# Eight deep visits: VectorE's order around the second layer's first four sums

## The chip, the cores and the metric

The kernel runs on one core of one Trainium2 chip. The metric is the device time of one execution in microseconds (us), lower is better. Three executions of the kernel before took 889.67, 889.99 and 894.23 us, median 889.99.

## The reference

Linear attention by random features, followed by a mixture of four two-layer experts in which every expert sees every token.

```python
# attention, per batch b and head h (4 x 8, 576 tokens, head size 64, 128 features)
phi(x) = exp(h - max(h)) / sqrt(m),   h = x @ omega.T - sum(x * x) / 2
kv = einsum('bhsm,bhsd->bhmd', phi(k), v);  z = sum(phi(k), axis=2)
out = (phi(q) @ kv) / (phi(q) @ z + 1e-6)

# experts: x is the attention output, 2304 tokens x 512; E = 4, F = 1024
p = probs / (probs.sum(-1) + 1e-9)
for e in range(E):
    out += p[:, e] * (relu(x @ w1[e]) @ w2[e])
```

## The kernel before, in words

Every float32 operand of a matmul is split into a high and a low part, and each product is three matmuls (high x high, high x low, low x high), which add up in PSUM. The work on the experts goes in *visits*: one visit takes one half of one expert's hidden units (eight halves in all) for one block of tokens. The last eight visits take the last block, 1024 tokens; the code calls them DEEP, and in them both layers are computed with seven block products in place of eight (a Strassen-like scheme). The function `fast(v)` writes a visit. The attention of later batches lies beside the earlier visits and is over by then.

The order on each engine is the order in which the code writes the instructions; no scheduler changes it, and waits are semaphores that follow from the tiles read and written. Two instructions on one PSUM bank by TensorE and VectorE are put in order too, even if they touch different halves of it.

A deep visit has two parts.

The first layer is 14 products (`p1` to `p7` for two groups g) of six matmuls, 128x512 each. `p4(1)`, the last one, ends with a ReLU whose high part ScalarE writes (L922) and whose low part VectorE writes (L925, `hl`). `both` adds a product to an earlier sum (L879) and writes low parts (L892).

The second layer, in `sevens()`, is seven groups of 24 matmuls, 128x256 each, six for each of four token tiles q. Four PSUM banks `X[q]` have a left half L and a right half R; two more banks hold `zs`. In TensorE's order the groups are:

- G1: L of X, from `hs[:2]` (laid between p7, p3 and p4 of the first layer)
- G2: R of X, from `T1`, added to what L's bank already holds
- G3: `zs`, from `hs[2:]`; its sixth matmul is the first that needs the low half `hl` of p4
- G4: R of X, from `A22`
- G5: L of X, from `hs[:2]`, written anew by ScalarE and GpSimd from `t2`
- G6: L of X, from `hs[2:]`, written anew from `r11`
- G7: L of X, from `T1`, written anew from `t1`

Because each group adds to what the bank holds, VectorE must have read a half of X[q] before the next group on this bank may write there: `gather` (L714 or L718) multiplies the half by the token's probability and adds it to an accumulator. `second(q)` is a gather of `zs`, `third(q)` one of R after G4.

Between them stand the differences that make the next operands, written by `less` (L857): `less(t2[:, 0], ...)` (tile `vb`, from sum and va), after which ScalarE and GpSimd split t2 (L498, L501) and GpSimd computes `r11 = t2 - r11` (L973, tile `r`); and two with the tile `va` as output, `less(t1[:, 1], P_[1]["u"], t2[:, 1])`, which reads PSUM and vb, and `less(t1[:, 0], P_[1]["p1"], t2[:, 0])`, which reads two tiles in SBUF, sum and vb.

Of the kernel before, what the change touches and what calls it, by code (L numbers as in the profile page):

```python
# [14 lines left out]
def attention_moe(ctx, tc, kT, qT, kd, qd, kn, qn, vn, omT, probs, w1, w2, out):  # L15
# [89 lines left out]
    def held(shape, tag, dtype=F32R, name=None):  # L105
        return moe.tile(shape, dtype, tag=tag, name=name or tag, bufs=BUFS[tag])
# [588 lines left out]
    def part(i, cs):  # L695
        if not isinstance(acc[i], list):
            return acc[i][:, cs]
        h = cs.start // H
        return acc[i][h][:, cs.start - h * H:cs.stop - h * H]

    def gather(v, ps, t, cs=slice(0, DM)):
        _, e, _, c0, n = visits[v]
        i = c0 // P + t
        sc = pr[:, i, e:e + 1]
        if i not in acc:
            if v in DEEP and t == 3:
                acc[i] = [att.tile([P, H], F32, tag=x, name="acc", bufs=1) for x in ("kvh", "kvl")]
            else:
                acc[i] = held([P, DM], "acc", F32)
        to = part(i, cs)  # L710
        fresh = [h for h in (0, H) if cs.start <= h < cs.stop and (i, h) not in begun_at]
        begun_at.update((i, h) for h in fresh)
        if fresh and v in DEEP:
            nc.vector.tensor_scalar(to, ps, sc, None, ALU.mult)  # L714
        elif fresh:
            nc.scalar.activation(to, ps, AF.Copy, scale=sc)
        else:
            nc.vector.scalar_tensor_tensor(to, ps, sc, to, ALU.mult, ALU.add)  # L718
# [57 lines left out]
    X = {}  # L776
# [51 lines left out]
    def fast(v):  # L828
# [27 lines left out]
        def less(to, t, x, op=ALU.subtract):  # L856
            nc.vector.scalar_tensor_tensor(to, t, 0.0, x, ALU.max, op)  # L857

        def product(g, p, where, start=True):
            if start:  # L860
                P_[g][where] = bank("g1")[:, :n]
            ps = P_[g][where]
            (wa, wc), (xa, xc) = W[v, "w1", g][p], X[p]
            for k in range(2):
                w = slice(k * P, (k + 1) * P)
                for a, x, at in ((wa, xa, 0), (wa, xc, 1), (wc, xa, 2)):
                    nc.tensor.matmul(  # L867
                        ps, a[:, w], x[:, k], start=(start and k + at == 0), stop=(k == 1 and at == 2), skip_group_check=not start
                    )
# [49 lines left out]
        def p4(g):  # L919
            product(g, 4, "u", start=False)  # L920
            ha, hc = (x[:, :n] for x in hs[2 * g + 1])
            nc.scalar.activation(ha, P_[g]["u"], AF.Relu)  # L922
            if deep and g == 0:
                nc.scalar.activation(r11[:, 1], P_[0]["u"], AF.Relu)
            nc.vector.scalar_tensor_tensor(hc, P_[g]["u"], 0.0, f32(ha), ALU.max, ALU.subtract)  # L925

        def p3(g):
            product(g, 3, "b5", start=False)
            both(g, 0, 1, "b5", "u2")
# [14 lines left out]
        def sevens():  # L944

            L, R, Q = slice(0, H), slice(H, DM), range(4)

            def split_of(t):
                return [tuple(x[:, f] for x in t) for f in range(2)]

            def weights(g, cs):
                return [tuple(x[:, cs] for x in W[v, "w2", 2 * g + f]) for f in range(2)]

            def mixed(i, cs):
                return [tuple(x[:, cs] for x in B[f, i]) for f in range(2)]

            X, Z = [], []
            for f in range(2):
                for q in Q[:2]:
                    if f == 0:  # L960
                        X.append(bank("g2"))
                    seventh(q, X[q][:, L], hs[:2], weights(0, L), fs=(f,))
            p7(1)
            less(t2[:, 1], P_[1]["p5"], t1[:, 1])
            for q in Q[2:]:
                X.append(bank("g2"))
                seventh(q, X[q][:, L], hs[:2], weights(0, L))
            split(t2[:, 1], *hs[1], nc.scalar, nc.gpsimd)
            p3(1)
            less(t2[:, 0], P_[1]["u2"], t1[:, 0])  # L970
            p4(1)
            split(t2[:, 0], *hs[0], nc.scalar, nc.gpsimd)
            nc.gpsimd.tensor_tensor(r11, t2, r11, ALU.subtract)  # L973
            for q in Q:
                seventh(q, X[q][:, R], split_of(T1), mixed(1, R), start=False)
            for q in Q:
                gather(v, X[q][:, L], q, L)
                gather(v, X[q][:, R], 4 + q, R)
            yield 2
            zs = []  # L980
            for q in Q:
                if q % 2 == 0:
                    Z.append(bank("g2"))
                zs.append(Z[q // 2][:, q % 2 * H:(q % 2 + 1) * H])
                seventh(q, zs[q], hs[2:], weights(1, L))
            for f in range(2):
                split(r11[:, f], *hs[2 + f], nc.scalar, nc.gpsimd)
            yield 2
            for q in Q:
                seventh(q, X[q][:, R], split_of(A22), mixed(1, L), start=False)  # L990

            def second(q):
                gather(v, zs[q], q, L)
                finished(v, q, L)

            def third(q):
                gather(v, X[q][:, R], 4 + q, L)

            second(0)
            third(0)  # L1000
            less(t1[:, 1], P_[1]["u"], t2[:, 1])
            third(1)
            less(t1[:, 0], P_[1]["p1"], t2[:, 0])
            third(2)
            second(1)
            third(3)
            split(t1, *T1, nc.scalar, nc.gpsimd)
            next(ready, None)
            next(ready, None)
            on_sides2(v + 1)  # L1010
            yield 1
            for q in Q:
                seventh(q, X[q][:, L], hs[:2], mixed(0, L), start=False)
                gather(v, X[q][:, L], 4 + q, L)
                finished(v, 4 + q, L)
                if q < 2:
                    second(2 + q)
            next(ready, None)
            on_sides2(v + 1)
            on_sides2(v + 1)  # L1020
            yield 1
            for q in Q:
                seventh(q, X[q][:, L], hs[2:], mixed(0, R), start=False)
                gather(v, X[q][:, L], 4 + q, R)
                finished(v, 4 + q, R)
            on_sides2(v + 1)
            yield 1
            for q in Q:
                seventh(q, X[q][:, L], split_of(T1), weights(1, R), start=False)
                gather(v, X[q][:, L], q, R)  # L1030
                finished(v, q, R)
            for t in range(tiles):
                gathered(v, t)
            yield 1
# [359 lines left out]
```

## Time and profile before

| what | value |
|---|---|
| timed runs, median (lowest to highest) | 889.99 us (889.67 to 894.23) |
| span of the profiled execution | 890.8 us |
| granted TensorE clock, mean | 1.000 |
| PE busy | 884.1 us, 99% |
| VectorE (DVE) busy | 593.8 us, 67% |
| ScalarE (ACT) busy | 468.9 us, 52% |
| GpSimd (POOL) busy | 566.3 us, 64% |
| the eight deep visits on TensorE | 571.13 to 887.52 us |

The profiled execution's span of 890.8 us is 0.8 us above the median of the timed runs; the profile gives no other time of its own for that execution. Times in the rows below count from the start of this span. A matmul that overlaps the one before it counts as busy for its whole duration, so the distance between the starts of matmuls says more than the busy time.

### The profile page before, as it was taken

The numbers are of one execution on the slowest core, as the hardware profiler recorded it, in microseconds if no ns is written. First come the engines' busy times: TensorE is split into PE (matmuls) and PEld (weight loads), VectorE is DVE, ScalarE is ACT, GpSimd is POOL, SyncE is SP. The second block draws the span as 40 slices with busy tenths as digits, with TensorE's granted clock in tenths as the row PEclk, the third lists the DMA queues.
The fourth block names the chain that finished last, engine by engine and source line by source line (L and its number), as shares of the span: only waits on it lengthen the run. The fifth ranks groups of instructions, "written<-read, shape, count | busy, mean of one in ns | idle before, by whom it ended". The sixth has DMA issues, their size and how long they took to land.

```text
span 890.8 us, 14823 instructions
## 1 busy us (share of the span) xinstructions
PE 884.1 (99%) x5484; PEld 789.4 (89%) x5484; DVE 593.8 (67%) x1026; ACT 468.9 (53%) x1038; POOL 566.3 (64%) x494
## 2 busy tenths in 40 slices
PE   9999999999999999999999999999999999999998
PEld 9988888888888898989889899898989898998988
DVE  5765566766767646586766666975848476675847
ACT  5564676776774564546545554634443435444442
POOL 6656465555634554444445346779898888979874
PEclk9999999999999999999999999999999999999999
DMA  6664454444521757436275353835152442425132
GB/s 179 165 204 153 127 170 135 150 154 137 160 80 60 254 154 274 181 135 246 77 273 175 111 211 111 305 117 165 48 178 87 139 157 80 155 60 178 44 135 95
DMA packets 64552, 134.01 MB, mean 150 GB/s; under 512 B 10624, under 2 KB 21056, under 8 KB 64480
## 3 DMA queue, kind: packets, MB, share of 16 engines
q1 hardware_dynamic: 54512, 102.95, 35.3%
q0 software_dynamic: 9360, 29.82, 10.3%
q8 instruction: 43, 0.70, 0.3%
q10 hardware_dynamic: 608, 0.30, 0.1%
q14 instruction: 29, 0.24, 0.1%
HBM read 98.96 MB, written 34.08 MB: 149 GB/s over the span
## 4 chain that ended last, share of the span: by engine, by line
PE 90%; DVE 4%; issue 2%; DMA 2%; ACT 1%; POOL 1%; SPq 0%; POOLq 0%; ACTq 0%; DVEq 0%
PE g L867 26%; PE g L942 17%; PE g L689 8%; PE g L691 7%; PE g L690 7%; PE g L674 3%; PE g L676 3%; PE g L675 3%; PE kv L314 2%; PE q_ps L266 1%; PE k_ps L266 1%; DMA kept<-w1ah 1%; PE qt_ps L325 1%; PE k_ps L147 1%; PE q_ps L147 1%
## 5 line engine op out<-in xcount | busy, mean ns | idle before, releaser
L501 POOL TENSOR_TENSOR w2l<-w2r,w2h 128x512 fp32r<-128x512 f32 x93 | 123.9, 1337 | 81.6 <-ACT w2h L498 69.8
L718 DVE SCALAR_TENSOR_TENSOR acc<-g,pr,acc 128x256 f32<-128x256 f32 (+1 forms) x278 | 139.2, 539 | 31.7 <-PE g L691 21.8
L501 POOL TENSOR_TENSOR w1sl<-w1r,w1sh 128x512 fp32r<-128x512 f32 (+1 forms) x43 | 75.2, 1749 | 72.3 <-ACT w1sh L498 56.8
L689 PE MATMUL g<-w2h,hh 128*128 128x512 f32 x280 | 112.7, 402 | 0.4 <-ACT kp L296 0.2
L691 PE MATMUL g<-w2h,hl 128*128 128x512 f32 x280 | 109.8, 392 | 0.0
L690 PE MATMUL g<-w2l,hh 128*128 128x512 f32 x280 | 109.5, 391 | 0.0
L879 DVE TENSOR_TENSOR sum<-g,sum 128x384 f32<-128x384 f32 (+1 forms) x96 | 59.3, 619 | 63.1 <-PE g L867 56.4
L892 DVE SCALAR_TENSOR_TENSOR hl<-sum,hh 128x384 fp32r<-128x384 f32 (+1 forms) x64 | 45.7, 717 | 81.7 <-ACT hh L888 52.3
L867 PE MATMUL g<-xbh,w1sh 128*128 128x384 f32 (+1 forms) x256 | 93.1, 364 | 0.0
L867 PE MATMUL g<-xbl,w1sh 128*128 128x384 f32 (+1 forms) x256 | 92.9, 363 | 0.0
L867 PE MATMUL g<-xbh,w1sl 128*128 128x384 f32 (+1 forms) x256 | 92.6, 362 | 0.0
L501 POOL TENSOR_TENSOR w1al<-w1r,w1ah 128x512 fp32r<-128x512 f32 (+1 forms) x45 | 51.5, 1159 | 52.1 <-ACT w1ah L498 36.7
L873 ACT ACTIVATE sum<-g 128x384 f32<-128x384 f32 (+1 forms) x96 | 50.7, 541 | 51.9 <-PE g L867 51.0
L867 PE MATMUL g<-xbh,w1ah 128*128 128x384 f32 (+1 forms) x192 | 70.1, 365 | 0.0
L498 ACT ACTIVATE w2h<-w2r 128x512 fp32r<-128x512 f32 x90 | 55.2, 627 | 28.2 <-DMA w2r<-in_w 22.1
L867 PE MATMUL g<-xbl,w1ah 128*128 128x384 f32 (+1 forms) x192 | 69.6, 362 | 0.0
L867 PE MATMUL g<-xbh,w1al 128*128 128x384 f32 (+1 forms) x192 | 69.5, 362 | 0.0
L691 PEld LDWEIGHTS g<-w2h,hl 128*128 128x128 f32 x280 | 52.5, 188 | 11.9 <-DVE hl L925 0.4
L689 PEld LDWEIGHTS g<-w2h,hh 128*128 128x128 f32 x280 | 52.7, 188 | 11.2 <-DVE sum L879 0.7
L690 PEld LDWEIGHTS g<-w2l,hh 128*128 128x128 f32 x280 | 52.7, 188 | 8.7
L888 ACT ACTIVATE hh<-sum 128x384 fp32r<-128x384 f32 (+1 forms) x64 | 35.0, 550 | 41.6 <-DVE sum L879 41.2
L867 PEld LDWEIGHTS g<-xbh,w1sh 128*128 128x128 f32 x256 | 48.1, 188 | 6.0 <-DVE sum L879 0.6
(212 smaller groups left out, 2438.5 us busy)
## 6 DMA issues: line engine op xcount, KB each, us to landing
w2r<-in_w SPq DMA_DIRECT2D x108, 256.0 KB, 2.9
w1r<-in_w SPq DMA_DIRECT2D x38, 512.0 KB, 3.6
kept<-w1sh SPq DMA_DIRECT2D x16, 512.0 KB, 4.9
kept<-w1sl SPq DMA_DIRECT2D x16, 512.0 KB, 5.5
w1sh<-kept POOLq DMA_DIRECT2D x16, 512.0 KB, 5.8
w1sl<-kept POOLq DMA_DIRECT2D x16, 512.0 KB, 6.6
kept<-w1ah SPq DMA_DIRECT2D x16, 384.0 KB, 4.3
kept<-w1al SPq DMA_DIRECT2D x16, 384.0 KB, 4.5
```

The lines of the kernel that those rows point to most:

```text
L498: hi.activation(a, t, AF.Copy)
L501: lo.tensor_tensor(c, t, f32(a), ALU.subtract)
L689: nc.tensor.matmul(ps, ha[:, ts_], wa, start=(c == 0), stop=False)
L690: nc.tensor.matmul(ps, ha[:, ts_], wc, start=False, stop=False)
L691: nc.tensor.matmul(ps, hc[:, ts_], wa, start=False, stop=(c == FH - 1))
L718: nc.vector.scalar_tensor_tensor(to, ps, sc, to, ALU.mult, ALU.add)
L867: nc.tensor.matmul(ps, a[:, w], x[:, k], start=(start and k + at == 0), stop=(k == 1 and at == 2), skip_group_check=not start)
L873: nc.scalar.activation(t, P_[g][where], AF.Copy)
L879: nc.vector.tensor_tensor(t, P_[g][where], t, ALU.add)
L888: nc.scalar.activation(ha, t, AF.Relu)
L892: nc.vector.scalar_tensor_tensor(x, y, 0.0, f32(z), ALU.max, ALU.subtract)
L942: nc.tensor.matmul(to, x, w, start=(start and f + k == 0), stop=(f + k == 3), skip_group_check=not start)
```

## The change

Only `sevens()` changes, and in it only where VectorE's instructions stand. No instruction is added or taken away on any engine; TensorE, ScalarE, GpSimd and the DMA queues keep their order. Three things move.

```diff
             split(t2[:, 1], *hs[1], nc.scalar, nc.gpsimd)
             p3(1)
+            p4(1)
             less(t2[:, 0], P_[1]["u2"], t1[:, 0])
-            p4(1)
             split(t2[:, 0], *hs[0], nc.scalar, nc.gpsimd)
             nc.gpsimd.tensor_tensor(r11, t2, r11, ALU.subtract)
             for q in Q:
                 seventh(q, X[q][:, R], split_of(T1), mixed(1, R), start=False)
             for q in Q:
-                gather(v, X[q][:, L], q, L)
                 gather(v, X[q][:, R], 4 + q, R)
...
-            second(0)
-            third(0)
             less(t1[:, 1], P_[1]["u"], t2[:, 1])
-            third(1)
             less(t1[:, 0], P_[1]["p1"], t2[:, 0])
-            third(2)
-            second(1)
-            third(3)
+            for q in Q:
+                gather(v, X[q][:, L], q, L)
+                third(q)
             split(t1, *T1, nc.scalar, nc.gpsimd)
...
                 seventh(q, X[q][:, L], hs[:2], mixed(0, L), start=False)
                 gather(v, X[q][:, L], 4 + q, L)
                 finished(v, 4 + q, L)
-                if q < 2:
-                    second(2 + q)
+                if q:
+                    second(q - 1)
+            second(3)
```

The first place is on VectorE in the fifth deep visit, from the sum of p3 on; `hl_8264` is the low half of p4, `vb_79` is t2, and `g2_8404`, `8408`, `8428` and `8435` are the banks X[0] to X[3]. Before:

```order
L879 TENSOR_TENSOR sum_8394<-g1_8356,sum_8394 128x512
L892 SCALAR_TENSOR_TENSOR t_hl_6567<-sum_8394,t_hl_6567 128x512
L857 SCALAR_TENSOR_TENSOR vb_79<-sum_8394,va_78 128x512
L925 SCALAR_TENSOR_TENSOR hl_8264<-g1_8318,hh_8263 128x512
L718 SCALAR_TENSOR_TENSOR acc_6808<-g2_8404,pr_76,acc_6808 128x256
L718 SCALAR_TENSOR_TENSOR acc_6810<-g2_8404,pr_76,acc_6810 128x256
L718 SCALAR_TENSOR_TENSOR acc_6812<-g2_8408,pr_76,acc_6812 128x256
L718 SCALAR_TENSOR_TENSOR acc_6814<-g2_8408,pr_76,acc_6814 128x256
```

After, the same place; the low half and the difference have changed places, and the four gathers of R stand alone, with the two differences into `va_78` right behind them:

```order
L879 TENSOR_TENSOR sum_8394<-g1_8356,sum_8394 128x512
L892 SCALAR_TENSOR_TENSOR t_hl_6567<-sum_8394,t_hl_6567 128x512
L925 SCALAR_TENSOR_TENSOR hl_8264<-g1_8318,hh_8263 128x512
L857 SCALAR_TENSOR_TENSOR vb_79<-sum_8394,va_78 128x512
L718 SCALAR_TENSOR_TENSOR acc_6808<-g2_8404,pr_76,acc_6808 128x256
L718 SCALAR_TENSOR_TENSOR acc_6810<-g2_8408,pr_76,acc_6810 128x256
L718 SCALAR_TENSOR_TENSOR acc_6812<-g2_8428,pr_76,acc_6812 128x256
L718 SCALAR_TENSOR_TENSOR acc_6814<-g2_8435,pr_76,acc_6814 128x256
L857 SCALAR_TENSOR_TENSOR va_78<-g1_8318,vb_79 128x512
L857 SCALAR_TENSOR_TENSOR va_78<-sum_8325,vb_79 128x512
```

The accumulators are handed out in another order too, so that their numbers differ; nothing hangs on that. The second place is on the same engine a little later, around the two differences into `va_78`; `g2_8497` holds the first half of `zs`. Before:

```order
L718 SCALAR_TENSOR_TENSOR acc_6808<-g2_8497,pr_76,acc_6808 128x256
L718 SCALAR_TENSOR_TENSOR acc_6810<-g2_8404,pr_76,acc_6810 128x256
L857 SCALAR_TENSOR_TENSOR va_78<-g1_8318,vb_79 128x512
L718 SCALAR_TENSOR_TENSOR acc_6814<-g2_8408,pr_76,acc_6814 128x256
L857 SCALAR_TENSOR_TENSOR va_78<-sum_8325,vb_79 128x512
L718 SCALAR_TENSOR_TENSOR acc_6818<-g2_8428,pr_76,acc_6818 128x256
L718 SCALAR_TENSOR_TENSOR acc_6812<-g2_8497,pr_76,acc_6812 128x256
L718 SCALAR_TENSOR_TENSOR acc_6823<-g2_8435,pr_76,acc_6823 128x256
```

After, from the second of these differences on; behind it come eight gathers, two of each bank X[q] (L, then R), and none of `zs`:

```order
L857 SCALAR_TENSOR_TENSOR va_78<-sum_8325,vb_79 128x512
L718 SCALAR_TENSOR_TENSOR acc_6872<-g2_8404,pr_76,acc_6872 128x256
L718 SCALAR_TENSOR_TENSOR acc_6808<-g2_8404,pr_76,acc_6808 128x256
L718 SCALAR_TENSOR_TENSOR acc_6875<-g2_8408,pr_76,acc_6875 128x256
L718 SCALAR_TENSOR_TENSOR acc_6810<-g2_8408,pr_76,acc_6810 128x256
L718 SCALAR_TENSOR_TENSOR acc_6878<-g2_8428,pr_76,acc_6878 128x256
L718 SCALAR_TENSOR_TENSOR acc_6812<-g2_8428,pr_76,acc_6812 128x256
L718 SCALAR_TENSOR_TENSOR acc_6881<-g2_8435,pr_76,acc_6881 128x256
L718 SCALAR_TENSOR_TENSOR acc_6814<-g2_8435,pr_76,acc_6814 128x256
```

The four gathers of L have moved behind the differences, and all four gathers of `zs` have moved behind the gathers of G5.

## Rows read from the trace of the kernel before

**Rows 1.** Busy time by stretch: deep visits one, three, five, eight; sum of all eight.
```profile
core 0: us, PE busy (x) PEld busy (x) DVE busy (x) ACT busy (x) POOL busy (x), PEclk, DMA share, GB/s
571.13:610.17 39.04, 39.04 (x253) 35.70 (x253) 31.77 (x50) 16.58 (x28) 33.41 (x29) 1.00 0.38 124
...
650.79:689.91 39.12, 39.12 (x253) 35.78 (x253) 25.33 (x46) 16.59 (x28) 34.17 (x32) 1.00 0.38 122
...
729.83:769.47 39.64, 39.60 (x254) 35.87 (x253) 27.08 (x46) 16.70 (x28) 34.57 (x32) 1.00 0.38 121
...
848.45:887.52 39.07, 39.05 (x253) 35.50 (x251) 25.52 (x46) 14.57 (x24) 25.77 (x19) 1.00 0.30 100
sum 316.39, PE 315.50 PEld 286.26 DVE 215.82 ACT 131.19 POOL 267.23; mean PE 39.44 PEld 35.78 DVE 26.98 ACT 16.40 POOL 33.40
```

**Rows 2.** Waits of TensorE's weight loads, 571 to 891 us.
```profile
engine line waited for: us in total, times, longest us
PEld g L942 <- DVE hl L925: 1.3, 3, 0.7
PEld g L942 <- DVE acc L718: 1.1, 5, 0.2
```

**Rows 3.** TensorE in order of time, fifth deep visit: start, duration, form.
```profile
754.97 0.28 PE L942 MATMUL g<-w2l,hh 128*128 128x256 f32 x1
755.22 0.39 PE L942 MATMUL g<-w2h,hl 128*128 128x256 f32 x1
755.45 0.28 PE L942 MATMUL g<-w2h,hh 128*128 128x256 f32 x1
...
757.58 3.01 PE L942 MATMUL g<-w2s,t_hl 128*128 128x256 f32 x24
760.43 0.40 PE L942 MATMUL g<-w2s,hh 128*128 128x256 f32 x2
...
762.04 0.50 PE L942 MATMUL g<-w2s,hh 128*128 128x256 f32 x2
...
763.62 0.40 PE L942 MATMUL g<-w2s,hh 128*128 128x256 f32 x2
```

**Rows 4.** VectorE in order of time, same visit, from the low parts of p3 on.
```profile
752.58 1.38 DVE L892 SCALAR_TENSOR_TENSOR t_hl<-sum,t_hl 128x512 fp32r<-128x512 f32 x1 [0.70 <-ACT t_hl L888]
753.89 0.68 DVE L857 SCALAR_TENSOR_TENSOR vb<-sum,va 128x512 f32<-128x512 f32 x1
754.49 0.68 DVE L925 SCALAR_TENSOR_TENSOR hl<-g,hh 128x512 fp32r<-128x512 f32 x1
755.09 3.99 DVE L718 SCALAR_TENSOR_TENSOR acc<-g,pr,acc 128x256 f32<-128x256 f32 x10
759.01 0.67 DVE L857 SCALAR_TENSOR_TENSOR va<-g,vb 128x512 f32<-128x512 f32 x1
759.61 0.47 DVE L718 SCALAR_TENSOR_TENSOR acc<-g,pr,acc 128x256 f32<-128x256 f32 x1
760.00 1.59 DVE L857 SCALAR_TENSOR_TENSOR va<-sum,vb 128x512 f32<-128x512 f32 x1
761.51 4.92 DVE L718 SCALAR_TENSOR_TENSOR acc<-g,pr,acc 128x256 f32<-128x256 f32 x12
```

**Rows 5.** GpSimd in order of time, same visit, with idle before and its releaser.
```profile
752.11 1.31 POOL L501 TENSOR_TENSOR hl<-vb,hh 128x512 fp32r<-128x512 f32 x1 [0.94 <-ACT hh L498]
755.31 1.31 POOL L501 TENSOR_TENSOR hl<-vb,hh 128x512 fp32r<-128x512 f32 x1 [1.89 <-ACT hh L498]
756.57 2.44 POOL L973 TENSOR_TENSOR r<-vb,r 128x1024 f32<-128x1024 f32 x1
759.75 2.99 POOL L501 TENSOR_TENSOR hl<-r,hh 128x512 fp32r<-128x512 f32 x2 [0.74 <-ACT hh L498]
```

**Rows 6.** VectorE in order of time, two differences of the first layer.
```profile
705.30 0.68 DVE L857 SCALAR_TENSOR_TENSOR va<-sum,r 128x512 f32<-128x512 f32 x1
...
745.23 1.23 DVE L857 SCALAR_TENSOR_TENSOR va<-sum,r 128x512 f32<-128x512 f32 x1
```

**Rows 7.** GpSimd in order of time, beside those two differences.
```profile
705.32 1.27 POOL L552 TENSOR_TENSOR w2f<-w2f,w2r 128x256 f32<-128x256 f32 x1
...
745.16 0.74 POOL L552 TENSOR_TENSOR w2f<-w2f,w2r 128x256 f32<-128x256 f32 x1
```

**Rows 8.** GpSimd in order of time, first layer of the sixth deep visit.
```profile
780.11 2.59 POOL L501 TENSOR_TENSOR w2s<-w2f,w2s 128x512 fp32r<-128x512 f32 x2 [0.56 <-ACT w2s L498]
...
787.21 2.44 POOL L501 TENSOR_TENSOR t_hl<-va,t_hl 128x1024 fp32r<-128x1024 f32 x1 [0.57 <-ACT t_hl L498]
```

## The prediction, made before the changed kernel ran

> **What bounds the kernel now.** The change touches the eight deep visits alone, so I read these 316.39 us first, visit by visit [rows 1]. The shortest visit takes 39.04 us on TensorE and the clock is granted in full; if each of the eight took that, they would last 312.32 us. So 316.39 - 312.32 = 4.07 us, 0.46% of the whole, is all that TensorE loses here by waiting, and no reordering of VectorE can give back more. Next I read what the losses are [rows 2]: matmuls that wait for the low half of p4 (`hl`, L925), three times, 1.3 us, and matmuls that wait for a gather (L718), five times, 1.1 us. Then the fifth visit engine by engine.
>
> There the two waits lie in G3 and G5 [rows 3]. In G3 the sixth matmul starts 0.25 us behind the fifth, where the step is else 0.12, and the next step is 0.23: 0.13 + 0.11 = 0.24 us lost. In G5 the third tile starts at 762.04. A group of 24 steps takes 760.43 - 757.58 = 2.85 us, 0.71 per tile; G5 takes 763.62 - 760.43 = 3.19, so 0.34 is lost, about half of it behind the wait, where the first steps are slow again. Together 0.6 us, the visit's excess over 39.04 [rows 1].
>
> What is late is VectorE [rows 4]. The low half is computed at 754.49 and ends at 755.17; its matmul starts at 755.22. The third tile of G5 waits for `third(2)`, the gather at 761.51: 762.04 - 761.51 = 0.53 us from its start to the matmul. That gather stands behind `less(t1[:, 0], ...)`, which takes 1.59 us at 760.00 where its like takes 0.68.
>
> Why 1.59: GpSimd runs a subtraction from 759.75 on [rows 5]. The first instance of this is clearer: the low parts at 752.58 last until 753.96, 0.54 us behind the end of GpSimd's instruction (752.11 + 1.31 = 753.42) [rows 4, 5]. A VectorE instruction whose two tensor inputs both lie in SBUF waits until a running GpSimd subtraction is over. With one input in PSUM (0.67 us at 759.01, the gathers at 0.39 a step beside the 2.44 us of L973) it doesn't.
>
> **The change, part by part.** I count from 753.89, where VectorE is free after the low parts of p3. This point hangs on what lies ahead of the change and stays.
>
> *Low half of p4 first.* `hl` starts at 753.89 in place of 754.49. Its matmul could go at 754.62 and TensorE comes there at 755.09: the wait in G3 goes, -0.24 us in this visit. Its price: `vb` starts 0.60 later, and with it ScalarE's and GpSimd's chain behind it. From `vb` to L973 the rows give 756.57 - 753.89 = 2.68 us, so L973 now starts at 754.49 + 2.68 = 757.17 and, at 2.44 us, ends at 759.61.
>
> *Gathers of R ahead of those of L.* Four gathers in place of eight stand between `vb` and what follows. G4 needs them at 757.34; they are over by 755.09 + 4 x 0.39 + 0.08 = 756.7. They have waited for no one before, and gain nothing now.
>
> *Two differences ahead.* After the four gathers (10 of them take 759.01 - 755.09 = 3.92 us, so 1.57) the first difference starts at 756.66, reads PSUM, and takes a step of 0.60. The second, with both inputs in SBUF, is thus up at 757.26. L973 has started at 757.17, 0.09 us ahead of it. Where both come close together the rows show who wins: a difference that starts 0.07 behind GpSimd's start (745.23 against 745.16) takes 1.23 us, and one that starts 0.02 ahead (705.30 against 705.32) takes 0.68 and GpSimd is stretched to 1.27 [rows 6, 7]. By this the second difference waits for the whole of L973: until 759.61, and ends at 759.61 + 0.54 = 760.15, with the next gather started 0.08 ahead of that, at 760.07 (as 761.51 stands to 760.00 + 1.59).
>
> No row shows such a difference held by L973 itself, so the price has two ends: 0, if L973 doesn't hold VectorE, and 2.44 - 0.09 = 2.35 us of delay. The nearest rows are the other GpSimd subtractions, which all hold it; I take 2.35.
>
> *What waits then.* G5 needs for tile q both gathers of its bank. They start at 760.07 + 0.39 steps, the second of tile q at 760.46, 761.25, 762.03 and 762.81, and 0.53 later TensorE may go: 760.99, 761.78, 762.56, 763.34. Without waits, and with G3 mended, TensorE is at G5 at 760.43 - 0.24 = 760.19. So it waits 0.8 us for tile 0, loses about 0.1 to 0.2 behind the wait, follows VectorE tile by tile (0.78 against 0.71 us) and ends G5 at 763.34 + 0.71, with slow steps about 764.1. Before it ended at 763.62. The visit grows by about 0.45 us.
>
> *Gathers of `zs` later.* All four now stand behind G5's. Behind `third(3)` at 762.81 VectorE has eight more gathers (four of G5, four of `zs`), so G6's first gather starts at 763.20 + 8 x 0.39 = 766.34, and G7's first tile may go at 766.87. TensorE comes there at 764.1 + 2.85 = 766.95: it just fits, at no cost; without this 0.08 us of cover it costs a wait. In the last visit these gathers also release stores to memory, some 3 us later than before but still ahead of G7's, which end the kernel: nothing.
>
> *Other visits.* From `vb` on all the late visits run to one time table, so 0.45 us holds for the five with the gather's wait [rows 2], 2.25 us. The third, where TensorE waits for almost nothing (39.12), ends G5 as late: +0.4. In the eighth (39.07) TensorE reaches G5 later of itself, so it loses less: +0.25. The first is not on this table (GpSimd is behind with other work): 0. Sum +2.9 us.
>
> Something comes back. GpSimd's chain is 0.60 later at `r11`, but its next split is no longer cut in two by the difference (2.99 us for two of 1.27 each [rows 5], 0.42 regained). So it runs about 0.2 us later while TensorE runs 0.45 later, and where GpSimd's lateness delays the next visit's first layer, up to 0.25 us per visit is returned, in up to four visits: 0 to 1.0. I take +2.3 us.
>
> The profiled execution would go from 890.8 to 893.1 us; the timed median lies 0.8 below that span, so 889.99 + 2.3 = 892.3 us.
>
> The trace shows GpSimd and VectorE holding each other up for whole instructions. The Trainium skill (SBUF — State Buffer, section "SBUF: two separate sides") says that the port which the two share is an exclusive lock, given for the whole instruction to whichever starts first, and that a VectorE instruction with two SBUF inputs takes part against a GpSimd one that reads SBUF. By that rule L973, which reads two SBUF tiles and starts 0.09 ahead, would hold the difference to its end, and the sum is the one above: the rule speaks against this change. With the starts the other way round the same rule gives the first rival.
>
> **Rivals.** *The difference wins the port (faster).* The margin is 0.09 us, and sums of five rows can be off by that. If it starts first, it ends by 757.94, L973 is 0.55 us late, and the pairs of gathers follow G4 tile by tile; the last pair is read at about 761.3, a microsecond ahead of G5's last tile, and both waits go in all visits. That is 4.07 us less the waits in the second visit's first layer (about 0.4): -3.6. Against it, GpSimd's chain is 0.60 + 0.55 - 0.42 = 0.7 us later per visit, and TensorE 0.6 earlier. Its slack in the sixth visit is 0.56 + 0.57 = 1.1 us [rows 8], so it takes some back: -2.5 us, 887.5 us. The same gain, without L973's delay, if L973 holds nothing: -3.5 us, 886.5.
>
> *The backlog spills over (slower).* If the difference is held and the gathers of `zs` make G6 and G7 wait too, the price is decided at G7's first tile, which has 0.08 us to spare. If VectorE is another 0.1 us behind, G6 and G7 each wait once, and each wait costs its length and some 0.17 of slow steps: 0.35 us more in seven visits, 2.5, and nothing comes back: 889.99 + 2.9 + 2.5 = 895.4 us.
>
> *Nothing shows.* If GpSimd's part gives back more than I allow, the sum can fall to about +0.5: 890.5 us.
>
> **How the numbers follow.** Difference held: 0.60. Difference first: 0.22; L973 holds nothing: 0.05. Spill: 0.09. Nothing: 0.04. A measurement can tell about 0.5% here, 4.45 us: under 885.5 is faster, over 894.4 slower. The two gaining cases reach 886.5, and no case can gain more than the 4.07 us, so faster has 0.03, for the error of measuring; slower has the spill and a little of the main case's tail, 0.09; within 0.5% the rest, 0.88. The main case alone runs from +1.4 to +3.2 with some 0.5 of measurement: 890.9 to 893.7. The range that holds 8 in 10 takes in the first rival: 886.8 to 893.8.
>
> **What would show it.** In the profile after, in the late visits: L925 waits in G3 gone; L973 about 3.28 us behind the point where `hl` starts; the second difference into `va` some 2.9 us long and ending 0.54 behind L973; TensorE waiting for L718 at G5's first tile, 0.6 to 1.3 us; visits of 39.5 to 40.5 us, no G6 or G7 waits. Wrong it is if that difference takes 0.68 us: then visits near 39.1 and a faster kernel. A wait of G5 for POOL or ACT would mean that I followed the wrong chain.

## The result, and the profile after

The changed kernel takes 894.9 us, median of 10 runs (893.36 to 897.42), against 890.51 us of the kernel before in 10 runs beside them: ratio 1.0054, 95% interval 1.0044 to 1.0063. It is slower, as forecast, but by 4.4 us (the interval says 3.9 to 5.6) and not by 2.3. 894.9 lies 1.1 us above the predicted range; 0.5 of that is the base, since the prediction counts from 889.99, a median of three runs, and the ten beside the changed kernel give 890.51.

The page of the changed kernel has a span of 895.1 us (890.8 before). First the deep visits on TensorE, with the columns of [rows 1]: visits one, two, five and eight.

```profile
570.77:611.23 40.46, 39.54 (x254) 35.99 (x253) 34.08 (x50) 16.58 (x28) 34.83 (x31) 1.00 0.41 130
611.23:651.15 39.92, 39.56 (x253) 35.94 (x253) 27.69 (x46) 16.46 (x28) 33.48 (x32) 1.00 0.37 120
...
731.43:771.56 40.13, 39.52 (x253) 35.97 (x253) 27.22 (x46) 16.48 (x28) 33.67 (x32) 1.00 0.37 116
...
851.60:891.23 39.63, 39.53 (x253) 35.78 (x251) 26.14 (x46) 14.35 (x24) 24.19 (x18) 1.00 0.26 88
sum 320.46, PE 316.27 PEld 287.55 DVE 225.04 ACT 129.94 POOL 261.29; mean PE 39.53 PEld 35.94 DVE 28.13 ACT 16.24 POOL 32.66
```

The sum went from 316.39 to 320.46: 4.07 us, nearly all of the 4.4 that the timed runs show, at full clock throughout. The first visit alone grew by 1.4. The waits of TensorE's matmuls from 571 to 896 us, and below them those of its weight loads, which answer to [rows 2]:

```profile
engine line waited for: us in total, times, longest us
PE g L942 <- DVE acc L718: 3.2, 6, 0.6
PE g L942 <- DVE acc L714: 0.9, 1, 0.9
```

```profile
PEld g L942 <- ACT hh L498: 5.6, 8, 1.1
```

Seven matmuls wait for a gather, and eight weight loads, one per visit; the low half of p4 (L925) is no longer among them. The weight loads name ScalarE's `hh`, but the matmul behind them is released later, by the gather. The fifth visit on VectorE, to be laid beside [rows 4]:

```profile
755.38 0.68 DVE L925 SCALAR_TENSOR_TENSOR hl<-g,hh 128x512 fp32r<-128x512 f32 x1
755.98 0.68 DVE L857 SCALAR_TENSOR_TENSOR vb<-sum,va 128x512 f32<-128x512 f32 x1
756.58 1.65 DVE L718 SCALAR_TENSOR_TENSOR acc<-g,pr,acc 128x256 f32<-128x256 f32 x4
758.15 0.67 DVE L857 SCALAR_TENSOR_TENSOR va<-g,vb 128x512 f32<-128x512 f32 x1
758.75 2.91 DVE L857 SCALAR_TENSOR_TENSOR va<-sum,vb 128x512 f32<-128x512 f32 x1
761.58 8.36 DVE L718 SCALAR_TENSOR_TENSOR acc<-g,pr,acc 128x256 f32<-128x256 f32 x21
```

GpSimd in the same stretch, which answers to [rows 5]:

```profile
757.40 1.31 POOL L501 TENSOR_TENSOR hl<-vb,hh 128x512 fp32r<-128x512 f32 x1 [2.49 <-ACT hh L498]
758.66 2.44 POOL L973 TENSOR_TENSOR r<-vb,r 128x1024 f32<-128x1024 f32 x1
761.85 2.54 POOL L501 TENSOR_TENSOR hl<-r,hh 128x512 fp32r<-128x512 f32 x2 [0.74 <-ACT hh L498]
```

L973 starts 0.09 us ahead of the second difference and ends at 761.10; the difference ends 0.55 us behind that. TensorE, to be laid beside [rows 3]:

```profile
756.69 0.28 PE L942 MATMUL g<-w2h,hl 128*128 128x256 f32 x1
756.81 0.28 PE L942 MATMUL g<-w2h,hh 128*128 128x256 f32 x1
...
758.97 3.01 PE L942 MATMUL g<-w2s,t_hl 128*128 128x256 f32 x24
762.59 0.48 PE L942 MATMUL g<-w2s,hh 128*128 128x256 f32 x2 [0.61 <-DVE acc L718]
```

G3 runs through in even steps of 0.12, and G5's first tile waits 0.61 us for a gather behind the difference. The first visit is another matter. VectorE there:

```profile
596.83 0.68 DVE L857 SCALAR_TENSOR_TENSOR va<-g,vb 128x512 f32<-128x512 f32 x1
597.43 3.88 DVE L857 SCALAR_TENSOR_TENSOR va<-sum,vb 128x512 f32<-128x512 f32 x1
```

And GpSimd:

```profile
594.69 0.56 POOL L642 DMA_DIRECT2D w1ah<-kept  x1
595.25 0.54 POOL L642 DMA_DIRECT2D w1al<-kept  x1
595.81 2.57 POOL L501 TENSOR_TENSOR hl<-vb,hh 128x512 fp32r<-128x512 f32 x2
598.35 2.41 POOL L973 TENSOR_TENSOR r<-vb,r 128x1024 f32<-128x1024 f32 x1
```

The difference comes up inside the second half of GpSimd's split. It doesn't get in when that ends (598.38), but only when L973 too is over (600.76).

### The profile page after: what moved, and what is told of

Its sections match the earlier page's. It is cut to its first block, busy times and chain, and to the rows that moved or that the text cites. A ratio compares the mean times of both kernels' runs of the same rounds, so it can differ in the third digit from the quotient of the medians.

```text
span 895.1 us, 14819 instructions
## 1 busy us (share of the span) xinstructions
PE 884.7 (99%) x5484; PEld 790.8 (88%) x5484; DVE 604.1 (67%) x1026; ACT 467.7 (52%) x1038; POOL 560.6 (63%) x494
## 4 chain that ended last, share of the span: by engine, by line
PE 81%; DVE 12%; ACT 2%; issue 2%; DMA 1%; POOL 0%; SPq 0%; ACTq 0%; POOLq 0%; DVEq 0%
PE g L867 25%; PE g L942 10%; PE g L689 7%; PE g L691 7%; PE g L690 7%; PE g L674 3%; PE g L676 3%; PE g L675 3%; DVE va L857 3%; PE kv L314 2%; DVE t_hl L892 2%; DVE acc L718 2%; PE q_ps L266 1%; PE k_ps L266 1%; PE qt_ps L325 1%
## 5 line engine op out<-in xcount | busy, mean ns | idle before, releaser
L501 POOL TENSOR_TENSOR w2l<-w2r,w2h 128x512 fp32r<-128x512 f32 x93 | 123.9, 1338 | 84.8 <-ACT w2h L498 72.1
L718 DVE SCALAR_TENSOR_TENSOR acc<-g,pr,acc 128x256 f32<-128x256 f32 (+1 forms) x278 | 136.4, 539 | 27.1 <-PE g L691 21.7
L501 POOL TENSOR_TENSOR w1sl<-w1r,w1sh 128x512 fp32r<-128x512 f32 (+1 forms) x43 | 75.6, 1758 | 70.7 <-ACT w1sh L498 54.6
L879 DVE TENSOR_TENSOR sum<-g,sum 128x384 f32<-128x384 f32 (+1 forms) x96 | 59.3, 619 | 62.6 <-PE g L867 55.9
L892 DVE SCALAR_TENSOR_TENSOR hl<-sum,hh 128x384 fp32r<-128x384 f32 (+1 forms) x64 | 46.8, 734 | 79.7 <-ACT hh L888 74.4
L501 POOL TENSOR_TENSOR w1al<-w1r,w1ah 128x512 fp32r<-128x512 f32 (+1 forms) x45 | 51.5, 1161 | 52.1 <-ACT w1ah L498 34.9
L873 ACT ACTIVATE sum<-g 128x384 f32<-128x384 f32 (+1 forms) x96 | 51.1, 541 | 53.6 <-PE g L867 52.7
```

Of the source, the lines that this page charges most:

```text
L501: lo.tensor_tensor(c, t, f32(a), ALU.subtract)
L873: nc.scalar.activation(t, P_[g][where], AF.Copy)
L879: nc.vector.tensor_tensor(t, P_[g][where], t, ALU.add)
L892: nc.vector.scalar_tensor_tensor(x, y, 0.0, f32(z), ALU.max, ALU.subtract)
```

## The experiments

"Sum" is that of the eight deep visits as the distance of TensorE's matmul starts, which a start that shifts as a whole doesn't disturb (568.5 to 571.1 us in these profiles). It is read from one execution each, the time is a median of 4 to 12 runs where the table doesn't say one. A ratio is to runs of the kernel before beside it, whose medians lie between 889.9 and 890.9, with its 95% interval.

| kernel | us | ratio | visits 1+2 | 3 to 8 | second difference, first visit / later |
|---|---|---|---|---|---|
| before | 890.5 | | 79.7 | 236.6 | 0.68 / 1.30 to 1.59 |
| before again | 891.6 | one run | 79.5 | 236.2 | |
| changed | 894.9 | 1.0054 [1.0044, 1.0063] | 80.4 | 240.0 | 3.88 / 2.90 |
| changed again | 894.2 | one run | 80.5 | 239.2 | 3.88 / 2.88 |
| e1 low half alone | 891.3 | 1.0011 [1.0000, 1.0023] | 78.2 | 237.8 | 0.68 / 0.68 |
| e2 gathers alone | 890.0 | 0.9995 [0.9984, 1.0006] | 80.0 | 235.4 | 3.33 / 2.30 |
| e3 difference late | 895.2 | 1.0057 [1.0039, 1.0074] | 78.9 | 240.1 | 0.96 / 1.09 to 1.37 |
| e4 r11 in halves | 895.4 | 1.0054 [1.0037, 1.0071] | 83.4 | 236.4 | 6.47 / 1.77 |
| e5 differences swapped | 893.7 | 1.0041 [1.0030, 1.0053] | 80.0 | 238.6 | 4.45 / 1.10 |
| e6 first visit as before | 893.8 | 1.0037 [1.0023, 1.0052] | 80.3 | 239.4 | |
| e7 e2 in visits 2 to 8 | 890.7 | 1.0007 [0.9994, 1.0020] | 79.6 | 234.9 | |
| e8 e7 and r11 in halves | 889.6 | 0.9991 [0.9980, 1.0002] | 80.1 | 234.4 | 3.18 / 1.17 |
| e9 DMAs behind r11 | 893.9 | 1.0047 [1.0032, 1.0063] | 80.5 | 239.5 | 0.90 / 2.90 |
| e10 best of these | 887.7 | 0.9975 [0.9963, 0.9987] | 78.9 | 234.8 | 0.68 / 1.18 |
| e13 work for the DMAs | 895.1 | one run | 80.9 | 239.4 | 1.59 / |
| e14 DMAs earlier | 894.4 | one run | 80.7 | 238.7 | 1.60 / |

**The two profiles again** (e11, e12: no edit).

> The kernel before once more, for a second profile of it. If the deep visits are the same from one execution to the next, their sum is 316.3 within 0.3 us and visits 2 to 8 take 277.2; if the second visit's 40.61 us was this one execution's, the sum comes out at 315 or less and the visits 2 to 8 at 276 or less, and the give-back that the comparison with the changed kernel read in the second visit is then not a property of the kernels.

> The changed kernel once more, for a second profile of it. If the deep visits are the same from one execution to the next, their sum is 320.3 within 0.3 us, visits 2 to 8 take 279.9, the second difference lasts 2.9 us in visits 2 to 8 and 3.9 us in the first. If the hold in the first visit was this one execution's, the difference there lasts 2 to 3 us and the sum is 319 or less.

A sum repeats to 0.7 us (315.69 and 316.26 before, 319.66 and 320.32 changed), not to the 0.3 expected, and visits 3 to 8 to 0.8, so smaller steps say nothing by one profile. The second visit is long again (40.45), and the hold in the first visit lasts 3.88 again: both are the kernel's own.

**Each part alone.** e1 is the kernel before with

```diff
+            p4(1)
             less(t2[:, 0], P_[1]["u2"], t1[:, 0])
-            p4(1)
```

> Only the first part of the change: the low half of p4 in front of the difference into vb; all gathers and the two differences into va stay where they were before. Theory (port): the second difference into va comes up about 6.1 us behind the point where the low half starts, L973 is over at 5.7 and GpSimd's next split starts at 6.5, so the difference takes 0.7 us in place of 1.6; the waits in G3 and in G5 both go: 2.0 to 3.5 us faster than before, 887 to 888.5 us. Rival (chain): what costs is that vb and with it GpSimd's chain are 0.6 us later; then this kernel loses most of what the whole change loses: 893 to 895 us. Rival (backlog): nothing but G3's wait goes, 889 us.

e2 is the changed kernel without these lines (L925 behind the difference again).

> The change without its first part: low half behind the difference into vb as before, but gathers and the two differences into va as in the changed kernel. Theory (port): L973 starts 2.7 us behind the start of vb, the second difference comes up at 3.4 us, well inside L973, and is held until 5.7 (2.3 us long in place of 2.9); G5's first tile may go 0.6 us earlier than in the changed kernel, about when TensorE comes there, G3's wait stays: near before, 890 to 892.5 us, with the first deep visit still slower by 0.5 to 1.5 us. Rival (backlog): the gathers' new places alone cost it, 894 to 895 us as the changed kernel.

Neither part costs much: e2's time is that of the kernel before, and e1's is at most 0.23% above it, with an interval that just touches 1. In e1 the second difference takes 0.68 us and the waits of [rows 2] are gone, but the gain expected from that doesn't come: the weight loads wait elsewhere, in the next visits' first layer:

```profile
PEld g L867 <- DVE sum L879: 2.5, 6, 0.5
PEld g L867 <- ACT sum L873: 1.6, 4, 0.5
```

In e2 the difference stands 0.69 us behind L973's start, not 0.09; it waits 0.6 us less, and in visits 2 to 8 the trace names no wait at G5. VectorE there, fifth visit:

```profile
754.90 2.30 DVE L857 SCALAR_TENSOR_TENSOR va<-sum,vb 128x512 f32<-128x512 f32 x1
```

So the loss belongs to the two parts together: the gathers' new order puts the difference into L973, and the low half moves L973's end 0.6 us later against TensorE.

**Is it the hold?** e3 moves the second difference out of L973, e4 cuts L973 in two, e5 puts the second difference in front of the first.

```diff
e3: -            less(t1[:, 0], P_[1]["p1"], t2[:, 0])     (in front of the eight gathers)
    +            less(t1[:, 0], P_[1]["p1"], t2[:, 0])     (behind them)
e4: -            nc.gpsimd.tensor_tensor(r11, t2, r11, ALU.subtract)
    +            for f in range(2):
    +                nc.gpsimd.tensor_tensor(r11[:, f], t2[:, f], r11[:, f], ALU.subtract)
e5: -            less(t1[:, 1], P_[1]["u"], t2[:, 1])      (first)
    +            less(t1[:, 1], P_[1]["u"], t2[:, 1])      (second)
```

> The changed kernel, but the second difference into va (both inputs in SBUF) stands behind the eight gathers of L and R, everything else as changed. Theory (port): nothing of VectorE that needs two SBUF inputs stands ahead of G5's gathers, so no visit waits at G5's first tile, the first one included; the difference meets GpSimd's splits of r11 instead and takes 0.7 to 1.9 us where only G6 and G7 hang on it: 886.5 to 889 us. Rival (backlog): gathers of L behind G4 and gathers of zs behind G5 make TensorE wait anyway: 893 to 895 us.

> The changed kernel, but GpSimd's r11 = t2 - r11 is two instructions of 128x512 in place of one of 128x1024. Theory (port, VectorE gets in between two GpSimd instructions): in deep visits two to eight the second difference is held by the first half alone, 1.8 us long in place of 2.9, G5's wait goes: 887 to 889 us. Theory (port, but two GpSimd instructions without a wait between them hold it through, as the 3.88 us in the first deep visit suggest): 2.9 to 3.1 us long, as the changed kernel, 894 to 896 us. Rival (backlog): 894 to 896 us too, with the difference short.

> The changed kernel with the two differences into va in the other order: the one that reads two SBUF tiles first. It comes up about 2.8 us behind the start of the low half, while GpSimd runs its split of vb (2.0 to 3.3), with L973 queued behind it. Theory A (a waiting VectorE instruction gets in at the end of the running GpSimd instruction): in visits two to eight it lasts about 1.1 us, L973 starts 0.5 us late, G5's wait goes: 888 to 890 us. Theory B (as in the first deep visit, 3.88 us, and 6.47 us with L973 in halves: an instruction that starts waiting during the split of vb is held until GpSimd runs dry): 3.4 to 3.6 us in every visit, as the changed kernel or a little slower, 894 to 896 us.

e4 is the clean test in the later visits. The difference gets in between the halves (fifth visit):

```profile
759.64 1.78 DVE L857 SCALAR_TENSOR_TENSOR va<-sum,vb 128x512 f32<-128x512 f32 x1
```

Visits 3 to 8 fall from 240.0 (239.2 in the second profile) to 236.4, where the kernel before has 236.6 and 236.2, and no matmul waits at G5 from the second visit on: there the length of the hold costs 2.8 to 3.6 us, all of the loss. (The long first visit is hardly what helps: the eighth is still free of the wait.) That e4 as a whole isn't faster comes from its first visit, 44.4 us long, where the difference is held for 6.47 us.

e3 missed its port theory: the long hold is gone (1.1 us and not 2.9), and the time stays where it was. `t1`, which comes out of the difference, is later through its new place than it was through the hold (in the fifth visit 8.3 us behind the start of the low half, 6.3 in the changed kernel), and TensorE waits in the first layer of the next visit; e3's weight loads:

```profile
PEld g L867 <- DVE sum L879: 1.7, 5, 0.4
PEld g L867 <- ACT sum L873: 1.6, 2, 1.2
```

For the longest of these waits, in the fourth visit, the trace shows another path than `t1`: ScalarE's L873 stands behind a split that waits for a weight transfer. SyncE issues the transfer, ScalarE goes on behind it:

```profile
687.35 6.41 SPq L494 DMA_DIRECT2D w2r<-in_w  x2
```

```profile
694.34 0.63 ACT L498 ACTIVATE w2h<-w2r 128x512 fp32r<-128x512 f32 x1 [4.75 <-DMA w2r<-in_w]
694.88 1.55 ACT L873 ACTIVATE sum<-g 128x512 f32<-128x512 f32 x3
```

The transfer overwrites a tile that GpSimd's split of the weights (L501, `w2l`) has to read first. It goes out 0.5 us behind the visit's start, in the changed kernel 1.2 us ahead of it: TensorE, without the wait at G5, is 1.1 us earlier against the low half of the visit ahead, and GpSimd, whose split of `r11` the difference now stretches from 2.54 to 3.00 us, 0.5 later. In e1 too it goes out 0.5 us behind the start, in each of visits 3 to 8, the ones whose first layer waits.

In e5 the difference lasts 1.10, since it gets in ahead of L973, and so holds GpSimd: L973 ends 6.16 us behind the start of the low half, not 5.72. The weight loads wait in the first layer again, 2.4 us for L873 and 1.7 for L879; in the fourth, seventh and eighth visit, which wait longest, the transfer goes out 0.55 to 0.59 us behind the start. What GpSimd is late by is paid for one visit later.

**The first visit.** e6 writes the first deep visit in the old order. e9 moves GpSimd's two DMA issues of that visit (L642) behind L973. e13 is e9 with a subtraction of their length in their old place. e14 has the issues in front of L551 to L554.

```diff
e6:  old = v == DEEP[0], then the lines before if old, else those after
e9, behind L973:  +            if v == DEEP[0]:
                  +                next(ready, None)
    and in front of sevens():
                  -            next(ready, None)
                  +            if v != DEEP[0]:
                  +                next(ready, None)
e13, to e9:  -            nc.gpsimd.tensor_tensor(s3, b11, b12, ALU.subtract)
             +            for _ in range(2 if v == DEEP[1] and f == 0 else 1):
             +                nc.gpsimd.tensor_tensor(s3, b11, b12, ALU.subtract)
e14, to the changed kernel:
    +            next(ready, None)
             if v == DEEP[0]:
                 start_sides2(v + 1)
    -            next(ready, None)
```

> The changed kernel, with the order of before in the first deep visit alone. Theory: that visit loses 1.4 us in the changed kernel, where its second difference is held for 3.88 us; with the old order it is back at 39.05 us: 1.0 to 1.6 us faster than the changed kernel, 893 to 894 us, the other seven visits as in the changed kernel (39.5 to 40.2 us). Rival: the lateness only moves to the second visit, whose first layer waits more (40.6 us as before): no gain, 894.5 to 895.5 us.

> The changed kernel, but in the first deep visit GpSimd issues the two weight DMAs (w1ah, w1al) behind r11's subtraction (L973) instead of directly in front of the low half of its split. Theory A (instructions of GpSimd that follow its DMA issues without a pause keep a waiting VectorE instruction out): the first visit's second difference lasts at most 3.0 us instead of 3.88, ends about 0.55 us behind the end of one GpSimd instruction, and the first visit takes 39.1 to 39.6 us instead of 40.45; the sum over the deep visits 319.2 to 319.6 if the second visit does not take the lateness over, and the time about 893.9. Theory B (the DMA issues have nothing to do with it, only that GpSimd does not pause): the difference lasts 3.5 to 4.0 us again, it ends behind L973, the first visit takes 40.3 to 40.6 us, and the time stays at 894.9.

> As the kernel with the two DMA issues behind r11, but where they stood in the first deep visit GpSimd writes the last quarter of w2f a second time (a 128x256 subtraction of about 1.2 us against 1.1 for the two issues), so that GpSimd's split and L973 stand against VectorE as in the changed kernel. Theory A (the DMA issues cause the long hold): the second difference gets in at the end of the second half of the split, lasts about 1.4 to 1.6 us, and the first visit takes 39.1 to 39.6 us. Theory B (GpSimd's unbroken run of instructions, and where the difference falls in it, causes it): the difference is held through L973 again, 3.8 to 4.0 us, and the first visit takes 40.3 to 40.6 us.

> The changed kernel with the two DMA issues of the first deep visit in front of the four preparations of w2f (L551 to L554) in place of directly behind them, 4.3 us earlier; GpSimd's split and L973 start where they did. Theory A1 (an issue keeps its effect until GpSimd pauses): the second difference is held through L973 again, 3.8 to 4.0 us, and the two-input VectorE instructions beside L551 to L554, 1.22 us in the changed kernel, are held longer too, 3 us or more. Theory A2 (only the first instructions behind an issue are concerned): the difference lasts 1.4 to 1.6 us and the first visit 39.1 to 39.6 us, unless VectorE was held earlier. Theory B (the issues do not matter): held, 3.8 to 4.0 us, and the VectorE instructions beside L551 to L554 as they were.

In e9 the difference lasts 0.90 us, but without the issues GpSimd's split starts 2.72 us ahead of it and not 1.62, so that e9 alone can't tell what did it. VectorE and then GpSimd in e13's first visit (from L554 on its line numbers are one higher):

```profile
595.70 1.59 DVE L858 SCALAR_TENSOR_TENSOR va<-sum,vb 128x512 f32<-128x512 f32 x1
```

```profile
593.10 1.11 POOL L555 TENSOR_TENSOR w2f<-w2r 128x256 f32<-128x256 f32 x1
594.17 2.57 POOL L501 TENSOR_TENSOR hl<-vb,hh 128x512 fp32r<-128x512 f32 x2
596.69 2.89 POOL L974 TENSOR_TENSOR r<-vb,r 128x1024 f32<-128x1024 f32 x1
```

The difference is up 1.53 us behind the split's start, as in the changed kernel (597.43 - 595.81 = 1.62). GpSimd is as busy, without a pause. The difference now gets in at the end of the split and stretches the subtraction behind it to 2.89. In e14 it does the same, and VectorE's instructions beside L551 to L554 last 1.22 and less. So, by one profile each of e13 and e14 against six with a hold, theory A holds: without the issues directly in front of the split, the run of instructions doesn't shut VectorE out over its boundaries. Whether A1 or A2 is right e14 doesn't show. In it one difference is up while the issues still run, on VectorE

```profile
589.34 1.22 DVE L857 SCALAR_TENSOR_TENSOR vb<-sum,va 128x512 f32<-128x512 f32 x1
```

and GpSimd

```profile
589.35 0.55 POOL L642 DMA_DIRECT2D w1al<-kept  x1
589.92 1.23 POOL L551 TENSOR_TENSOR w2f<-w2r 128x256 f32<-128x256 f32 x1
```

The difference is over at 590.56, before L551 is, so an instruction that waits already gets in directly behind the issues; in the kernels with the hold the difference came up later, inside an instruction behind them. A short reach behind the issues isn't the answer either, since in e8 the hold reaches to the end of the sixth instruction behind the issues; GpSimd stands still for 0.07 us between L551 and L552 in e14 (591.15 to 591.22), and whether such a pause is enough no run tells.

But the repaired first visit saves nothing: e6 and e9 bring it back to 39.06 us, and the second visit grows, to 41.2 and 41.4 from 39.9. Visits 1 and 2 take 80.3 to 80.9 in all four, 80.4 in the changed kernel. In these profiles the first visit's loss is one that the second would have had. The medians of e6 and e9 are 1.1 and 1.0 us lower, but the intervals overlap that of the changed kernel; e6's time lies where its theory put it, its visits where the rival did.

**A better kernel.** e7 is e2 with the old order in the first visit, e8 adds L973 in halves everywhere, e10 has the halves in visits 2 to 8 alone:

```diff
-            nc.gpsimd.tensor_tensor(r11, t2, r11, ALU.subtract)
+            for fs in [slice(0, 2)] if old else [slice(0, 1), slice(1, 2)]:
+                nc.gpsimd.tensor_tensor(r11[:, fs], t2[:, fs], r11[:, fs], ALU.subtract)
```

> The new places of gathers and differences, without the first part (low half behind the difference into vb as before), in deep visits two to eight; the first one in the order of before. Theory: visits two to eight take 274.5 to 275.5 us together (277.2 before) as in the kernel with gathers alone, the first 39.05: 2 to 2.5 us faster than before, 888 to 889 us. Rival: GpSimd sets the pace, and a first visit that is earlier makes the second wait: 889.5 to 890.5 us.

> As the kernel with the gathers' new places in deep visits two to eight alone, and r11 in two GpSimd instructions of 128x512. Theory: the second difference is held by the first half alone, about 1.1 us long in place of 2.3, the remaining waits at G5 (0.2 to 0.4 us in five visits) go, and GpSimd's chain is 0.5 us later because the difference gets in between the halves: 887.5 to 889 us, and no slower than with r11 in one piece. Rival: GpSimd sets the pace, its 0.5 us in seven visits comes back as waits in the next visit's first layer: 889.5 to 891 us.

> The old order in the first deep visit; in visits 2 to 8 the new place of the gathers and of the two differences, the low half of the fourth product behind the first difference as before, and r11's subtraction in two pieces of 128x512. Theory (what counts is how long the second difference is held by GpSimd, and the first visit alone holds it longest): first visit 39.05 us, second 40.5, the other six 39.1 each on the mean, sum 313.9 against 316.3 before, the difference about 1.2 us long in visits 2 to 8, the time 888.2, ratio 0.997 to 0.999. Rival (what the first visit saves, the second takes over, and the parts outside the deep visits drown the rest): sum 314.5 or more, ratio 0.9985 to 1.0005.

e7 and e8 show no gain that can be measured. e7's deep visits add up to 314.5 us, as expected, but its second visit still takes 40.5, and its twelve runs spread from 888.4 to 892.6, of which the profile shows one of 888.95. In e8's first visit the difference is held for 3.18 us.

e10 is faster than both kernels: 887.74 us, 0.13 to 0.37% under the kernel before. Its visits three and five, and the sum of all eight:

```profile
647.65:686.88 39.23, 39.23 (x254) 35.77 (x253) 26.00 (x46) 16.59 (x28) 34.19 (x33) 1.00 0.38 122
...
726.41:765.46 39.05, 39.05 (x254) 35.71 (x253) 25.29 (x46) 16.59 (x28) 34.39 (x33) 1.00 0.38 125
...
sum 313.87, PE 313.17 PEld 285.55 DVE 211.53 ACT 131.09 POOL 265.86; mean PE 39.15 PEld 35.69 DVE 26.44 ACT 16.39 POOL 33.23
```

39.05 is a visit without waits, and 313.87 is 1.55 us above eight times [rows 1]'s 39.04. Two L925 waits in G3 (1.1 us by the weight loads) are most of what is left. The sum and the second difference (1.17 to 1.18 us) came out as expected, and the time close to it (888.2).

## Why the prediction was wrong

**Right: the mechanism and its race.** The second difference was forecast to start 0.09 us behind L973, to last 2.9 us and to end 0.54 behind it. It starts 0.08 to 0.09 behind, lasts 2.89 to 2.92 and ends 0.54 to 0.55 behind, in all of visits 2 to 8; L973 stands 758.66 - 755.38 = 3.28 us behind the low half, as foreseen. L925's waits in G3 are gone, G5's first tile waits (0.4 to 0.6 us in visits 2 to 7, at or under the low end of the 0.6 to 1.3), and no G6 or G7 waits are named. Of the rivals, "the difference wins the port" and "nothing shows" are out. "The backlog spills over" gave 895.4, close to the time, but by waits in G6 and G7 that aren't there; its nearness is chance. All eight visits lie within the 39.5 to 40.5 us. One reading proves less than it says: the difference at 759.01 [rows 4], with one input in PSUM, runs when L973 is just over [rows 5]; but its like at 758.15 in the changed kernel takes 0.67 us beside GpSimd's L501 (757.40 to 758.71), so what was read from it holds.

**Mis-sized: "The visit grows by about 0.45 us".** From the point where VectorE is free (755.38 here, 753.89 before) to the next visit's start it is 771.56 - 755.38 = 16.18 us, against 769.47 - 753.89 = 15.58 [rows 1, 4]: 0.60. All of visits 2 to 8 show some 0.6, where I had five times 0.45, 0.4 for the third and 0.25 for the eighth: 4.1 us and not 2.9. The 0.15 us that are missing have three parts. My own G5 ended at "about 764.1", which is 0.48 behind 763.62 and not 0.45. G5 ends 0.05 later than that: TensorE starts it 0.62 us behind the pair's second gather (762.59 - (761.58 + 0.39)), where I let it start 0.53 behind by [rows 3, 4]. And G7's first step is slow, 0.18 us in place of 0.12, which makes that group 0.07 longer; I had no slow step there. The starts of G6 and G7 in the changed kernel:

```profile
765.64 0.40 PE L942 MATMUL g<-w2s,hh 128*128 128x256 f32 x2
...
768.47 0.35 PE L942 MATMUL g<-w2h,t_hl 128*128 128x256 f32 x1
768.65 0.28 PE L942 MATMUL g<-w2l,t_hl 128*128 128x256 f32 x1
```

And G7's before:

```profile
766.44 0.28 PE L942 MATMUL g<-w2h,t_hl 128*128 128x256 f32 x1
766.56 0.27 PE L942 MATMUL g<-w2l,t_hl 128*128 128x256 f32 x1
```

**Mis-sized: "up to 0.25 us per visit is returned".** I took 0.6 of it. The first layer, from a visit's start to that point, is 0.2 us shorter in visits 3 to 8 together. There was little to give back: in the kernel before, the trace names first-layer waits of TensorE (0.3 and 0.5 us) in the second visit alone. 1.3 more comes back in the second visit, but that is what the first had lost.

**Failed: "The first is not on this table (GpSimd is behind with other work): 0."** The visit took 1.4 us more. GpSimd's being behind doesn't keep the difference out of its way; behind two DMA issues the hold is longer than anything in [rows 4 to 7].

Together: 1.4 + 4.1 - 0.2 - 1.3 = 4.0 us (4.07 measured), against 0 + 2.9 - 0.6 = 2.3. Since the first visit's loss returns in the second, the error that counts is that of the first two points, and it lies in visits 3 to 8: 240.0 - 236.6 = 3.4 us, where my terms give 4 x 0.45 + 0.4 + 0.25 = 2.45 less what was to come back. The upper end of 893.8 let the main case cost at most 3.2 us, its own sum of 2.9 with little on top: an error of 0.15 us in a price that is paid seven times was not in it, nor one of 0.5 us in the base.

## What to carry to other kernels

When two engines hold each other up for whole instructions, look where the one that waits stands against the other's boundaries: six visits took 3.6 us less with the subtraction cut in halves, and 4.6 less with the subtraction 0.6 us earlier (one profile each, which repeats to 0.8). Try each part of such a change alone, since two moves that cost next to nothing by themselves lost 0.5% together. And when a wait is taken away, look at the next round: in e3 TensorE came sooner, GpSimd later, and the weights of the next visit, which wait for GpSimd, were late.

## What the runs showed of the hardware

- A waiting VectorE instruction with two SBUF inputs gets in at the end of GpSimd's running instruction and ends 0.54 to 0.55 us later (the 128x512 difference takes 1.10, 1.18, 1.77, 2.30 or 2.90 us, by how much of that was left). The Trainium skill (SBUF — State Buffer, section "SBUF: two separate sides") says that the port pair which the two share is a lock and goes to whichever starts first, for that whole instruction. The traces agree with it in visits 2 to 8; in the first visit of some kernels they don't:
- Where the difference comes up inside an instruction that follows two DMA issues of GpSimd without a pause, its wait goes over the boundaries, until GpSimd pauses: 3.88 us over one, 6.47 over four, in the first visits of the changed kernel, e2, e4, e5 and e8. With equal work in place of the issues: 1.59. Why is open, and so is how far behind the issues it reaches.
- After e4's wait of 3.47 us TensorE went on for 1.4 us as before and then for 3.4 us at the lower of its two levels (1.2 and 2.4 GHz), with steps of 0.21 us in place of 0.12; it worked on through both without a pause until the clock rose again. TensorE behind the wait, and the granted clock (third number from the end) of the three stretches behind the wait:

```profile
602.98 0.47 PE L942 MATMUL g<-w2s,hh 128*128 128x256 f32 x2 [3.47 <-DVE acc L714]
...
604.60 0.66 PE L942 MATMUL g<-w2s,hh 128*128 128x256 f32 x2
```

```profile
602.98:604.38 1.40, 1.40 (x11) 1.40 (x12) 1.40 (x5) 1.40 (x4) 1.16 (x1) 0.99 0.00 0
604.38:607.81 3.43, 3.43 (x18) 3.43 (x17) 3.15 (x9) 0.33 (x1) 3.43 (x6) 0.51 0.28 57
607.81:611.00 3.19, 3.19 (x29) 3.19 (x28) 2.73 (x7) 0.63 (x1) 3.17 (x4) 1.00 1.10 390
```

Behind e8's wait of 1.60 us at the same place the steps are 0.12 from the second matmul on, but for one of 0.19.
